# Gate and value in PSUM: three one-bank tiles in place of three slices of one tile, with a newly searched order

## The chip, the cores and the metric

The kernel runs on one core of one Trainium2 chip. The metric is the device time of one execution in microseconds (us). The time before is the median of three runs, 1481.7 us (1477.79 to 1482.69).

## What is computed

Three layers over 8192 tokens of 192 features, in float32:

```
w   = softmax(weight_gen)                        # per token, head and tap: 8 heads, 7 taps
x   = sum over taps of w * x at earlier tokens   # causal dynamic convolution
h   = x @ w_in                                   # 192 -> 2048
g   = (a0 + a1 h + a2 h^2 + a3 h^3) / (1 + |b0||h| + |b1| h^2 + 1e-6)
y   = g @ w_out                                  # 2048 -> 192
xn  = y / sqrt(mean(y^2) + 1e-6) * rms_g
out = (silu(xn @ w_gate) * (xn @ w_val)) @ w_out2   # 192 -> 1536 -> 192
```

## The kernel before, in words

The tokens are worked in 32 blocks (`b`) of 256 tokens. Products that need float32 are made from two float16 halves, so that one product of 192 features is five matmuls (`mm5`, line 837), and one of the second matrices three.

A block has two parts.

- **Rational part**, four quarters `q` of 512 columns each. `mm1` writes one PSUM tile `h` of two banks (two such tiles exist). ScalarE squares it (`tB`) and takes `|h|` (`tA`). VectorE makes the cubic in place in `h` (lines 875, 879), forms `g1h` (884) and the remainder (898), GpSimd forms `g1l` (902). The denominator is summed in one of three ways, chosen per quarter by the table `VAR` under `("qp", q)`: way 0 on VectorE (862), then ScalarE (889) and GpSimd (895); way 1 with one more ScalarE pass (856), then GpSimd (860) and GpSimd (895); way 2 on VectorE twice (862, 893). `mm2` multiplies `g1h` and `g1l` into the one bank `acc`.
- **Gate and value part**, six pieces `k` of 256 columns for gate and for value. `mm3` (ten matmuls at line 837) writes one bank of `gv`. There are three such banks, and the groups take them in turn, the gate and the value groups together. For a gate group ScalarE reads the bank with Silu and writes `gp` in SBUF (`silu`, line 984). For a value group VectorE multiplies bank and `gp` (`prod`, line 999); for four of the six pieces the product stays in the bank, ScalarE rounds it to float16 (`prod_hi`, line 1003) and VectorE takes the remainder (`prod_lo`, line 1007). After that the bank is free. `mm4` (line 1022) multiplies `gp` into `acc`.

Around these two parts GpSimd multiplies taps and inputs for the convolution of later blocks (373, 395), ScalarE makes the norm (925 to 957), and the first 140 us decode and split the weights. Silu and the exponentials need different ScalarE tables: a change between them is an ACT_TABLE_LOAD, issued ahead of a Silu or of an Ln.

Every engine takes its instructions in the order in which they were recorded. That order is a list of numbers, `RANK`, one per job (4777 jobs), found by a search outside the kernel. The waits between engines are set by the layer that records the program, by the tiles that instructions read and write. The search's own table of places, `CAPS`, counts three places for `gv`, before and after.

The lines that matter here:

```
late["gv"] = ... .tile([128, 3, NJ, 256], FP32, name="gv")     # gv_open, NJ = 2
gv[b, k, nm] = late["gv"][:, len(gv) % 3]                       # mm3
nc.scalar.activation(out=gp[b, k], in_=gv[b, k, "g"], func=ACTF.Silu, scale=silu_s)
nc.vector.tensor_tensor(out=l, in0=gv[b, k, "v"][:, 0:n16(k)], in1=h, op=ALU.subtract)
```

Of the kernel before, what the change touches and what calls it, by code (L numbers as in the profile page):

```python
# [10 lines left out]
FP32 = mybir.dt.float32  # L11
# [8 lines left out]
PSUM = bass.MemoryType.PSUM  # L20
# [3 lines left out]
def kernel(  # L24
# [31 lines left out]
    NJ = N2 // NK  # L56
# [69 lines left out]
    def c1(name):  # L126
# [702 lines left out]
    late = {}  # L829
# [141 lines left out]
    def gv_open():  # L971
        dec_ctx.__exit__(None, None, None)
        late["gv"] = ctx.enter_context(tc.tile_pool(name="ps_g", bufs=1, space=PSUM)).tile([128, 3, NJ, 256], FP32, name="gv")

    gv = {}

    def mm3(b, k, nm):
        gv[b, k, nm] = late["gv"][:, len(gv) % 3]
        for j in range(NJ):
            mm5(gv[b, k, nm][:, j, :], w3[nm, "A"], w3[nm, "B"], w3[nm, "C"], NJ * k + j, xnT[b])  # L980
# [49 lines left out]
    def store_out(b):  # L1030
# [507 lines left out]
```

## Time and profile before

| what | value |
|---|---|
| median of three runs | 1481.7 us |
| the profiled execution's own time | 1478.36 us |
| its span, first to last instruction | 1476.5 us |
| TensorE (PE) busy | 1248.8 us, 85% |
| VectorE (DVE) busy | 1222.8 us, 83% |
| ScalarE (ACT) busy | 1111.8 us, 75% |
| GpSimd (POOL) busy | 992.1 us, 67% |
| DMA engines busy, queue q1 | 12.8% |

The span runs from the first to the last instruction, the execution's own time is 1.9 us longer. The view by line gives for each group of instructions the busy time, the mean duration of one, the idle time of its engine just before them, and the engine and line that ended most of that idle time. The chain of work is followed back from the last instruction, at each step to what released it.

### The profile page before, as it was taken

The page shows a single profiled execution, that of the slowest core. Times are in us where ns is not written, and L with a number is a line of the kernel's source. Part 1 is how long each engine was busy: PE and PEld are TensorE (multiplying, and loading weights), DVE is VectorE, ACT ScalarE, POOL GpSimd, SP SyncE. Part 2 cuts the span into 40 slices and gives each one's busy share as a digit, 9 for nine tenths or more (in the row PEclk, how much of TensorE's full clock was granted, in tenths as well). Part 3 has the DMA queues.
Part 4 walks back from the last instruction along what each step waited for, and adds up shares of the span by engine and source line. Part 5 has one row for each costly group of instructions (what it writes and reads, how often), then busy time and mean ns, then how long its engine had stood idle before and what let it go on. Part 6 is the DMA issues. An engine that isn't in the chain of part 4 may idle for free.

```text
span 1476.5 us, 28197 instructions
## 1 busy us (share of the span) xinstructions
PE 1248.8 (85%) x11696; PEld 1122.1 (76%) x11696; DVE 1222.8 (83%) x1265; ACT 1111.8 (75%) x1521; POOL 992.1 (67%) x885
## 2 busy tenths in 40 slices
PE   3556788888899898998998888989888999988986
PEld 3455677777788787888887777878887888987876
DVE  5898788788888888978898979889887998987732
ACT  5878778777778778777787877778777888877832
POOL 6397678587857687776767677677665758675410
PEclk9887999999999999999999999999999999999999
DMA  7504420000002011002000021001010100000000
GB/s 256 166 22 97 112 90 18 20 20 17 12 9 60 15 49 31 12 15 60 14 15 15 7 63 18 15 21 33 28 25 7 26 12 23 17 18 12 17 7 16
DMA packets 69662, 55.02 MB, mean 37 GB/s; under 512 B 53791, under 2 KB 64543, under 8 KB 68638
## 3 DMA queue, kind: packets, MB, share of 16 engines
q1 hardware_dynamic: 66846, 49.18, 12.8%
q10 hardware_dynamic: 2688, 4.05, 0.8%
q8 instruction: 91, 1.49, 0.4%
q14 instruction: 37, 0.30, 0.1%
HBM read 31.72 MB, written 6.29 MB: 26 GB/s over the span
## 4 chain that ended last, share of the span: by engine, by line
PE 47%; DVE 23%; ACT 20%; issue 4%; POOL 4%; DMA 2%; DVEq 0%; SPq 0%; ACTq 0%; POOLq 0%
PE gv L837 23%; PE h L837 10%; ACT gp L984 6%; PE acc L1022 5%; DVE gv L999 3%; DVE tA L862 3%; DVE gp L1007 3%; PE acc L918 2%; PE acc L920 2%; PE acc L919 2%; DVE h L879 2%; DVE tA L898 2%; DVE g1h L884 2%; ACT gp L1003 2%; DVE h L875 2%
## 5 line engine op out<-in xcount | busy, mean ns | idle before, releaser
L902 POOL TENSOR_TENSOR g1l<-tA,tC 128x1024 f16<-128x1024 f32 x128 | 309.7, 2419 | 131.3 <-DVE tA L898 81.4
L918 PE MATMUL acc<-wo1h,g1h 128*128 128x192 f16 x992 | 245.9, 248 | 9.6 <-ACT y L925 6.7
L920 PE MATMUL acc<-wo1h,g1l 128*128 128x192 f16 x992 | 245.7, 248 | 7.1 <-POOL g1l L902 7.1
L919 PE MATMUL acc<-wo1l,g1h 128*128 128x192 f16 x992 | 245.8, 248 | 0.0
L837 PE MATMUL h<-xt,w1A 128*128 128x256 f16 x1024 | 221.4, 278 | 28.4 <-DVE tA L898 25.3
L837 PE MATMUL gv<-xnT,w3vA 128*128 128x256 f16 x768 | 174.6, 274 | 69.7 <-ACT gp L984 19.2
L837 PE MATMUL gv<-xnT,w3gA 128*128 128x256 f16 x768 | 170.3, 273 | 63.7 <-ACT gp L984 37.4
L1022 PE MATMUL acc<-wo,gp 128*128 128x192 f16 (+1 forms) x1920 | 221.8, 267 | 2.6 <-ACT osb L1028 2.5
L373 POOL TENSOR_TENSOR pt<-xc,wg 128x384 f32<-128x384 f32 x224 | 212.0, 991 | 1.4 <-DVE ac L389 0.5
L837 PE MATMUL h<-xt,w1C 128*128 128x256 f16 x1024 | 200.0, 278 | 0.0
L984 ACT ACTIVATE gp<-gv,silu_s 128x512 f32<-128x512 f32 x192 | 125.3, 686 | 94.3 <-PE gv L837 85.1
L884 DVE SCALAR_TENSOR_TENSOR g1h<-h,cf,tC 128x1024 f16<-128x1024 f32 x128 | 163.8, 1279 | 35.3 <-ACT tC L871 29.9
L875 DVE SCALAR_TENSOR_TENSOR h<-tB,cf,h 128x1024 f32<-128x1024 f32 x128 | 163.9, 1280 | 11.3 <-ACT tA L851 10.9
L898 DVE SCALAR_TENSOR_TENSOR tA<-h,cf,tA 128x1024 f32<-128x1024 f32 x128 | 163.6, 1278 | 3.1 <-POOL tA L895 1.4
L879 DVE SCALAR_TENSOR_TENSOR h<-tB,cf,h 128x1024 f32<-128x1024 f32 x128 | 164.0, 1281 | 1.9
L999 DVE SCALAR_TENSOR_TENSOR gv<-gp,val_h,gv 128x512 f32<-128x512 f32 x128 | 96.2, 752 | 68.1 <-PE gv L837 48.8
L851 ACT ACTIVATE tA<-h,cf 128x1024 f32<-128x1024 f32 x128 | 141.9, 1108 | 12.8 <-POOL g1l L902 6.0
L895 POOL TENSOR_TENSOR tA<-tA,g1h 128x1024 f32<-128x1024 f32 x54 | 115.4, 2138 | 51.2 <-DVE g1h L884 45.7
L871 ACT ACTIVATE tC<-tC,lnb 128x1024 f32<-128x1024 f32 x128 | 146.5, 1145 | 2.8
L837 PE MATMUL gv<-xnT,w3vC 128*128 128x256 f16 x768 | 147.6, 274 | 0.0
L837 PE MATMUL gv<-xnT,w3gC 128*128 128x256 f16 x768 | 147.0, 273 | 0.0
L847 ACT ACTIVATE tB<-h 128x1024 f32<-128x1024 f32 x128 | 129.9, 1015 | 20.8 <-PE h L837 20.7
(227 smaller groups left out, 3136.8 us busy)
## 6 DMA issues: line engine op xcount, KB each, us to landing
xc<-in_x_dram SPq DMA_DIRECT2D x7, 1344.0 KB, 6.4
out_dram<-osb SPq DMA_DIRECT2D x32, 192.0 KB, 2.0
xp<-in_x_dram SPq DMA_DIRECT2D x14, 384.0 KB, 3.3
raw<-in_moe_w_in_dram SPq DMA_DIRECT2D x6, 512.0 KB, 7.0
raw<-in_moe_w_out_dram SPq DMA_DIRECT2D x3, 768.0 KB, 4.5
wg<-in_weight_gen_dram SPq DMA_DIRECT2D x15, 112.0 KB, 2.0
raw<-in_moe_w_out_dram ACTq DMA_DIRECT2D x2, 768.0 KB, 8.6
raw<-in_moe_w_gate_dram SPq DMA_DIRECT2D x2, 768.0 KB, 4.9
```

The source lines that it names most:

```text
L373: nc.gpsimd.tensor_tensor(out=pt_t[b][:, :, :, k].rearrange("p i (h g) -> p i h g", h=NH), in0=xc_t[k0][:, o0 + k:o0 + k + 2, :].rearrange ...
L837: nc.tensor.matmul(out=dst, lhsT=w[:, fs], rhs=xt[:, :, c, :], start=(n == 0), stop=(n == 4))
L875: nc.vector.scalar_tensor_tensor(out=h, in0=tB[q], scalar=cf[:, 4:5], in1=h, op0=ALU.add, op1=ALU.mult)
L879: nc.vector.scalar_tensor_tensor(out=h, in0=tB[q], scalar=cf[:, 5:6], in1=h, op0=ALU.mult, op1=ALU.add)
L884: nc.vector.scalar_tensor_tensor(out=g1h[q], in0=hps[q], scalar=cf[:, 3:4], in1=tC[q], op0=ALU.add, op1=ALU.mult)
L898: nc.vector.scalar_tensor_tensor(out=tA[q], in0=hps[q], scalar=cfb(q)[:, 3:4], in1=tA[q], op0=ALU.add, op1=ALU.subtract)
L902: nc.gpsimd.tensor_tensor(out=g1l[q], in0=tA[q], in1=tC[q], op=ALU.mult)
L918: nc.tensor.matmul(out=acc[:, 0:D], lhsT=g1h[q][:, r, ts], rhs=wo1h[:, f, :], start=(f == 0), stop=False)
L919: nc.tensor.matmul(out=acc[:, 0:D], lhsT=g1h[q][:, r, ts], rhs=wo1l[:, f, :], start=False, stop=False)
L920: nc.tensor.matmul(out=acc[:, 0:D], lhsT=g1l[q][:, r, ts], rhs=wo1h[:, f, :], start=False, stop=(f == N1 - 1))
L984: nc.scalar.activation(out=gp[b, k], in_=gv[b, k, "g"], func=ACTF.Silu, scale=silu_s)
L1022: nc.tensor.matmul(out=acc[:, 0:D], lhsT=l, rhs=r, start=(f == 0 and n == 0), stop=(f == N2 - 1 and n == len(ops) - 1))
```

## The change

`gv_open` makes three tiles `gv0`, `gv1`, `gv2` of one bank each, where one tile `gv` of three banks stood, and `mm3` picks one of three tiles in place of one of three slices. The banks are as many and as large as before. `RANK` has new numbers, and `VAR` new ways for 17 quarters.

```
     def gv_open():
         dec_ctx.__exit__(None, None, None)
-        late["gv"] = ctx.enter_context(tc.tile_pool(name="ps_g", bufs=1, space=PSUM)).tile([128, 3, NJ, 256], FP32, name="gv")
+        pool = ctx.enter_context(tc.tile_pool(name="ps_g", bufs=1, space=PSUM))
+        late["gv"] = [pool.tile([128, NJ, 256], FP32, name=f"gv{i}") for i in range(3)]
...
     def mm3(b, k, nm):
-        gv[b, k, nm] = late["gv"][:, len(gv) % 3]
+        gv[b, k, nm] = late["gv"][len(gv) % 3]
...
-    RANK = [24, 28, 30, 37, 40, 44, 49, 56, 58, 61, 62, 63, 69, 73, 79, 82, 70, 80, 84, 91, 93, 94, 27, 32, 35, 39,
...
```

In `VAR` the quarters change as follows (old way, new way): 15, 70, 84: 0, 1; 25, 37, 43, 65: 2, 0; 38, 94: 1, 0; 56, 111: 0, 2; 92, 98, 106, 127: 2, 1; 96, 124: 1, 2. In all way 0 goes from 15 quarters to 16, way 1 from 39 to 42, way 2 from 74 to 70. The entry `('way', 'last')` that is added changes no instruction. Lines from 974 on stand one line lower in the changed kernel (984 is 985, 999 is 1000, 1003 is 1004, 1007 is 1008, 1500 is 1501).

The instructions that differ in number, counted in the recorded programs: line 856 and line 866 on ScalarE 39 to 42, line 868 there 89 to 86, line 889 there 15 to 16; table loads 47 to 50 ahead of Silu and 46 to 49 ahead of Ln; on VectorE line 862 89 to 86, line 893 74 to 70; on GpSimd line 860 39 to 42, line 895 54 to 58. All else is as many as before.

The order on VectorE at the end of the program, last two blocks, with the engine each row waits for (`gv_1118` is the one tile with three banks, `gv0` to `gv2` the three tiles; the names of `gp` buffers are numbered through). Before:

```order
L999 SCALAR_TENSOR_TENSOR gv_1118<-gp_16378,val_h_142,gv_1118 128x512 [waits Activation_49]
L1007 TENSOR_TENSOR gp_16368<-gv_1118,gp_16368 128x512 [waits DVE_49]
L999 SCALAR_TENSOR_TENSOR gv_1118<-gp_16429,val_h_142,gv_1118 128x512 [waits DVE_49,PE_49]
L1007 TENSOR_TENSOR gp_16429<-gv_1118,gp_16429 128x512 [waits Activation_49]
L1007 TENSOR_TENSOR gp_16378<-gv_1118,gp_16378 128x512 [waits Activation_49]
...
L999 SCALAR_TENSOR_TENSOR gv_1118<-gp_16717,val_h_142,gv_1118 128x512 [waits DVE_49,PE_49]
L1007 TENSOR_TENSOR gp_16717<-gv_1118,gp_16717 128x512 [waits PE_49,Activation_49]
```

and now:

```order
L1000 SCALAR_TENSOR_TENSOR gv0_1049<-gp_16437,val_h_142,gv0_1049 128x512 [waits PE_49]
L1008 TENSOR_TENSOR gp_16437<-gv0_1049,gp_16437 128x512 [waits Activation_49]
L1000 SCALAR_TENSOR_TENSOR gv2_1051<-gp_16450,val_h_142,gv2_1051 128x512 [waits PE_49]
L1008 TENSOR_TENSOR gp_16450<-gv2_1051,gp_16450 128x512 [waits Activation_49]
...
L1000 SCALAR_TENSOR_TENSOR gv0_1049<-gp_16753,val_h_142,gv0_1049 128x512 [waits PE_49]
L1008 TENSOR_TENSOR gp_16761<-gv2_1051,gp_16761 128x512 [waits Activation_49]
L1008 TENSOR_TENSOR gp_16753<-gv0_1049,gp_16753 128x512 [waits Activation_49]
```

`prod_lo` needs only `prod_hi` of ScalarE on its own bank. Before, 26 of its 128 instructions also wait for TensorE, which writes another bank; now none does. Of `prod_hi`, which needs only `prod` of VectorE, 51 of 128 waited for TensorE before and 3 do now.

The order on ScalarE some 45 rows before the end, around the last Silu of block 29. Before:

```order
L868 ACTIVATE tC_16271<-tA_16235,cf1_132 128x1024 [waits DVE_49]
L1003 ACTIVATE gp_16025<-gv_1118 128x512 [waits DVE_49,PE_49]
L871 ACTIVATE tC_16271<-tC_16271,lnb_160 128x1024 [waits Activation_49]
L1028 ACTIVATE osb_16057<-acc_16226,out_s_144 128x192 [waits PE_49]
L984 ACT_TABLE_LOAD [waits DVE_49]
L984 ACTIVATE gp_16340<-gv_1118,silu_s_141 128x512 [waits PE_49]
L984 ACTIVATE gp_16355<-gv_1118,silu_s_141 128x512 [waits DVE_49,PE_49]
L984 ACTIVATE gp_16368<-gv_1118,silu_s_141 128x512 [waits PE_49]
```

and now:

```order
L985 ACT_TABLE_LOAD [waits DVE_49]
L985 ACTIVATE gp_16336<-gv1_1050,silu_s_141 128x512 [waits PE_49]
L1501 ACT_TABLE_LOAD
L866 ACTIVATE tC_16291<-tA_16299 128x1024 [waits Pool_49]
L871 ACTIVATE tC_16291<-tC_16291,lnb_160 128x1024 [waits Activation_49]
L985 ACT_TABLE_LOAD
L985 ACTIVATE gp_16412<-gv1_1050,silu_s_141 128x512 [waits PE_49]
L985 ACTIVATE gp_16415<-gv0_1049,silu_s_141 128x512 [waits DVE_49]
```

Here one Silu is taken ahead of the last Ln and Exp, at two more table loads. The last quarter has gone from way 2 to way 1.

The first Silus of block 31, the last block, on the same engine, before:

```order
L984 ACTIVATE gp_16681<-gv_1118,silu_s_141 128x512 [waits PE_49]
L984 ACTIVATE gp_16693<-gv_1118,silu_s_141 128x512 [waits PE_49]
L984 ACTIVATE gp_16705<-gv_1118,silu_s_141 128x512 [waits PE_49]
L984 ACTIVATE gp_16717<-gv_1118,silu_s_141 128x512 [waits PE_49]
L1028 ACTIVATE osb_16719<-acc_16371,out_s_144 128x192 [waits DMAHW4_49]
```

and now:

```order
L985 ACTIVATE gp_16710<-gv1_1050,silu_s_141 128x512 [waits PE_49]
L985 ACTIVATE gp_16722<-gv0_1049,silu_s_141 128x512 [waits DVE_49]
L1004 ACTIVATE gp_16722<-gv2_1051 128x512 [waits DVE_49]
L985 ACTIVATE gp_16753<-gv1_1050,silu_s_141 128x512 [waits PE_49]
L985 ACTIVATE gp_16761<-gv0_1049,silu_s_141 128x512
```

Before, six Silus stood in a row, the first four of block 31 last among them; now a value piece's `prod_hi` (line 1004) is taken between the gates.

## Rows read from the trace of the kernel before

**Rows 1.** The page, part 1: busy time of the engines over the span.

```profile
PE 1248.8 (85%) x11696; PEld 1122.1 (76%) x11696; DVE 1222.8 (83%) x1265; ACT 1111.8 (75%) x1521; POOL 992.1 (67%) x885
```

**Rows 2.** The page, part 4: the chain that ended last, by line.

```profile
PE gv L837 23%; PE h L837 10%; ACT gp L984 6%; PE acc L1022 5%; DVE gv L999 3%; DVE tA L862 3%; DVE gp L1007 3%; PE acc L918 2%; PE acc L920 2%; PE acc L919 2%; DVE h L879 2%; DVE tA L898 2%; DVE g1h L884 2%; ACT gp L1003 2%; DVE h L875 2%
```

**Rows 3.** The view by line, the groups around `gv` and `h`.

```profile
L837 PE MATMUL h<-xt,w1A 128*128 128x256 f16 x1024 | 221.4, 278 | 28.4 <-DVE tA L898 25.3 <-ACT h L512 2.8
...
L837 PE MATMUL gv<-xnT,w3vA 128*128 128x256 f16 x768 | 174.6, 274 | 69.7 <-ACT gp L984 19.2 <-DVE gp L1007 17.8 <-DVE gv L999 15.6
L837 PE MATMUL gv<-xnT,w3gA 128*128 128x256 f16 x768 | 170.3, 273 | 63.7 <-ACT gp L984 37.4 <-DVE gp L999 16.7 <-DMA xnT<-xn 4.8
...
L984 ACT ACTIVATE gp<-gv,silu_s 128x512 f32<-128x512 f32 x192 | 125.3, 686 | 94.3 <-PE gv L837 85.1 <-DVE gp L999 7.4 <-DVE gp L1007 1.2
```

**Rows 4.** Waits: engine, line, what was waited for: us in total, times, longest.

```profile
ACT gp L1003 <- PE gv L837: 24.8, 25, 2.6
...
DVE gp L1007 <- PE gv L837: 12.7, 14, 2.1
```

**Rows 5.** The view of tile `gv`: who waited for its users (us, times).

```profile
  PE gv L837: 127.0, 149
```

**Rows 6.** Timeline of TensorE: start, length, instruction, idle before; block 0 and block 31.

```profile
155.32 0.27 PE L837 MATMUL gv<-xnT,w3gA 128*128 128x256 f16 x1 [0.78 <-ACT gp L984]
...
1438.19 0.27 PE L837 MATMUL gv<-xnT,w3gA 128*128 128x256 f16 x1 [0.78 <-ACT gp L984]
...
1439.17 0.27 PE L837 MATMUL gv<-xnT,w3gA 128*128 128x256 f16 x1
1440.22 0.27 PE L837 MATMUL gv<-xnT,w3gA 128*128 128x256 f16 x1 [0.78 <-ACT gp L984]
...
1463.49 0.27 PE L837 MATMUL gv<-xnT,w3vA 128*128 128x256 f16 x1 [1.04 <-ACT gp L1003]
```

**Rows 7.** Timeline of ScalarE beside it, block 31.

```profile
1437.46 0.69 ACT L984 ACTIVATE gp<-gv,silu_s 128x512 f32<-128x512 f32 x1 [1.34 <-PE gv L837]
1439.48 0.69 ACT L984 ACTIVATE gp<-gv,silu_s 128x512 f32<-128x512 f32 x1 [1.34 <-PE gv L837]
```

**Rows 8.** Busy time by stage: start:end, length, PE, PEld, DVE, ACT, POOL, then clock.

```profile
0.00:140.00 140.00, 71.44 (x494) 62.65 (x495) 114.66 (x176) 102.82 (x127) 93.18 (x88) 0.85 0.45 138
140.00:300.00 160.00, 134.01 (x1193) 116.03 (x1191) 133.28 (x171) 122.25 (x164) 114.61 (x96) 0.94 0.23 59
300.00:1300.00 1000.00, 898.13 (x8656) 813.37 (x8654) 871.70 (x818) 786.45 (x1081) 719.07 (x646) 1.00 0.10 24
1200.00:1300.00 100.00, 95.32 (x936) 87.57 (x935) 88.49 (x82) 87.19 (x116) 70.36 (x61) 1.00 0.06 15
1300.00:1476.50 176.50, 145.20 (x1362) 130.02 (x1359) 103.14 (x103) 100.30 (x151) 65.28 (x58) 0.99 0.06 14
```

**Rows 9.** The view by line, what the new ways of the quarters add and remove.

```profile
L862 DVE SCALAR_TENSOR_TENSOR tA<-tB,cf,tA 128x1024 f32<-128x1024 f32 x89 | 133.7, 1503 | 6.2 <-ACT tA L851 3.7 <-ACT tB L847 2.4
...
L895 POOL TENSOR_TENSOR tA<-tA,g1h 128x1024 f32<-128x1024 f32 x54 | 115.4, 2138 | 51.2 <-DVE g1h L884 45.7 <-ACT tA L889 5.3
L893 DVE SCALAR_TENSOR_TENSOR tA<-tA,cf,g1h 128x1024 f32<-128x1024 f32 x74 | 105.6, 1426 | 1.5
...
L860 POOL TENSOR_TENSOR tA<-tA,tC 128x1024 f32<-128x1024 f32 x39 | 92.0, 2359 | 67.8 <-ACT tC L856 53.2 <-ACT tA L851 14.3
...
L1500 ACT ACT_TABLE_LOAD x46 | 59.0, 1283 | 0.8
...
L856 ACT ACTIVATE tC<-tB,cf 128x1024 f32<-128x1024 f32 x39 | 48.3, 1239 | 1.4 <-POOL g1l L902 0.9
...
L889 ACT ACTIVATE tA<-tA,cf 128x1024 f32<-128x1024 f32 x15 | 17.1, 1143 | 0.2
```

**Rows 10.** One line's instructions, VectorE 862 and 898: duration in ns, min/median/max.

```profile
L862 DVE SCALAR_TENSOR_TENSOR tA<-tB,cf,tA x89: 1256/1284/3391, 58.5 to 1393.7; 128x1024 f32<-128x1024 f32 x89
...
L898 DVE SCALAR_TENSOR_TENSOR tA<-h,cf,tA x128: 1185/1279/1285, 65.8 to 1409.5; 128x1024 f32<-128x1024 f32 x128
```

572 rows, old and new, of tables (RANK, VAR) are left out of this document.

## The prediction
> **What bounds the kernel now.** I read the page first. No engine is full: TensorE is busy 85% of the span, VectorE 83%, ScalarE 75%, GpSimd 67% [rows 1]. The stages say where: TensorE has 71.4 of the first 140 us, 134.0 of the next 160, 898.1 of the 1000 us from 300 to 1300, and 145.2 of the last 176.5 [rows 8]. In the long middle no other engine is closer to full: VectorE 871.7, ScalarE 786.5, GpSimd 719.1 of 1000.
>
> Then the chain of waits: TensorE's `gv` groups hold 23% of it, with the three readers of `gv` at 6, 3, 3 and 2% (Silu, `prod`, `prod_lo`, `prod_hi`) [rows 2]. So the chain runs again and again from TensorE through a reader of `gv` back to TensorE. The view by line gives the price on TensorE: 69.7 us idle before value groups and 63.7 before gate groups, 133.4 in all, against 28.4 before the `h` groups [rows 3]. Of it, 127.0 us in 149 places waited for a reader of `gv` [rows 5].
>
> **Are these waits for the bank that is needed?** Three banks should let TensorE fill one while the others are read. In block 31 they don't. A gate group starts at 1438.19, its last matmul at 1439.17; Silu starts at 1439.48; the next gate group starts at 1440.22, after 0.78 us idle that ended with that Silu [rows 6, 7]. Silu's own idle time of 1.34 us ended with TensorE. The two engines strictly alternate, at 2.03 us a step (1438.19 to 1440.22), as if there were one bank. The bank taken at 1440.22 was last read three groups earlier and was long free.
>
> Two more rows cannot come from the right bank at all: `prod_hi` waits 24.8 us for TensorE, `prod_lo` 12.7 us [rows 4], though each needs only the step before it on VectorE or ScalarE. The recorded order agrees: 51 and 26 of 128 of them carry a wait for TensorE, since the waits go by the tile and the three banks are one tile.
>
> **The change, part by part.**
>
> *Three tiles.* With a tile per bank, a group waits only for the readers of the group three before it. I went through the 384 groups and took, for each, its start less the later of two ends, each with 0.06 us for the hand-over: that of the matmul ahead, and that of the last reader of its own bank. In 152 places the group starts later than both; the sum is 95.8 us: nothing before 140 us, 11.5 (19 places) from 140 to 300, 63.1 (106) from 300 to 1300, 21.2 (27) after. The first over half a microsecond is at 155.32, the last at 1463.49 [rows 6]. The other 37 or so of the 133.4 us are true waits for a bank, hand-overs and the transposed input's DMA. So this term is **-95.8 us** on TensorE's path. Its bounds: 0, if another wait takes its place each time, and -133.4, if all idle time before `gv` goes.
>
> *What is late next.* The middle would then last 1000 - 63.1 = 936.9 us with TensorE at 898.1 / 936.9 = 95.9%. The row nearest to that is the stretch from 1200 to 1300, where TensorE already reaches 95.3% with VectorE at 88.5% and ScalarE at 87.2% [rows 8]. So the kernel can feed TensorE at that rate. VectorE would be at some 92%, ScalarE at 85%, GpSimd at 78%. They too lose the false waits (the 37.5 us above among them), so I give nothing back.
>
> *The new ways of 17 quarters.* VectorE loses three instructions of line 862 at 1.503 us and four of line 893 at 1.426: -10.2 us. GpSimd gains three of line 860 at 2.359 and four of line 895 at 2.138: +15.6. ScalarE gains three of line 856 at 1.239, one of 889 at 1.143, and six table loads at 1.283: +12.6 [rows 9]. All of it lies beside TensorE in the middle, ScalarE and GpSimd having over 130 us idle there after the cut. I take 0, with -10 (VectorE's share on the path) and +13 (ScalarE's) as bounds. No DMA and no matmul is added or removed.
>
> *The new order.* It moves jobs on every engine, and the trace of before has no row for it. In the first 140 us the same decoding has to be done, with TensorE idle 68.6 us; one tenth of that either way, 7 us, is my bound. At the end, Silus and values alternate where six Silus stood in a row; the false waits there are already counted. I take 0.
>
> **Sum.** The profiled execution took 1478.4 us, 1.9 more than its span; 1478.4 - 95.8 = 1382.6. The median of the runs is 3.3 us higher, so for the median 1481.7 - 95.8 = 1385.9: I forecast **1386 us**, 6.5% less. Its own range is 1366 to 1406: the bounds of ways and order added, 20 either way.
>
> **A rule against it.** Line 862, two inputs in SBUF, has a median of 1.284 us but a mean of 1.503 and a maximum of 3.391, while line 898, one input in PSUM, never exceeds 1.285 [rows 9, 10]. Over 89 and 74 instructions of lines 862 and 893 that is some 30 us above the median. The Trainium skill (SBUF — State Buffer, section Who interferes with whom) says that a VectorE instruction with two SBUF inputs contends with a GpSimd instruction that reads SBUF; the rows agree. By that rule a denser schedule stretches VectorE more: with the 30 us grown as GpSimd's share does, from 72 to 78%, the sum would be some 2 us higher, and 30 us higher if they doubled. I leave it out of the sum.
>
> **Rivals.**
>
> *A: derived waits go as well (0.17).* VectorE's and ScalarE's delays also make TensorE wait for `h`. From 1200 to 1300, 3.1 of TensorE's 4.7 idle us are false waits by the count above; without them it would be busy 98.4%. With that in the whole middle, 898.1 / 0.984 = 912.7, a gain of 87.3, with 11.5 and 21.2 from the other stages 120: 1362 us. For it: `RANK` was searched with three free places, which the program has only now. Against: VectorE would have to reach 95%.
>
> *B: VectorE becomes the bound (0.20).* If VectorE keeps the 88.5% of that best stretch, the middle lasts (871.7 - 10.2) / 0.885 = 973 us, a gain of 27; with 11.5 and 21.2 it is 59: 1422 us. For it: VectorE is nearly as busy as TensorE, and its stretched instructions above. Against: part of VectorE's own idle time is false waits too, 12.7 us at `prod_lo` alone [rows 4].
>
> *C: slower (0.04).* The wait moves on to `h`, and ScalarE comes on the path: TensorE's idle time before `h` [rows 3] would grow from 28 to over 120 us, all that is gained at `gv`, because every `h` is freed only after ScalarE's Ln and Exp. Then ScalarE's added 12.6 us count in full: 1481.7 + 12.6 = 1494. It decides if ScalarE is above some 90% in the middle; it stands at 79% [rows 8], which speaks against.
>
> *D: no change (0.04).* The waits stay, under another name, 1482. The recorded order speaks against: no `prod_lo` waits for TensorE any more, and 3 of 128 `prod_hi`.
>
> **How the numbers follow.** The forecast has 0.55. Faster by over 0.3%, about what a measurement of this kernel can tell from no change: forecast, A and B, 0.92. Within it: D, 0.04. Slower: C, 0.04. The range goes from 1345 (A less VectorE's 10 us and 7 of the start) to 1430 (B with some 8 us, most of ScalarE's added work); C, D and the tails beyond A and B, in all about 2 in 10, are outside.
>
> **What would show it.** Right: TensorE's idle time before `gv` at 30 to 50 us instead of 133; no row of `prod_hi` or `prod_lo` waiting for TensorE above 2 us; in the last block, gate groups that follow each other in under 1.3 us where no `mm4` stands between; TensorE at 95 to 97% from 300 us on. A shows as over 97% there. B shows as TensorE waiting for `h` from line 898 for 60 us or more, VectorE below 90%. The forecast is wrong if the wait before `gv` falls below 50 us and the time does not fall by 59 us, or if it stays above 100.

## The result and the profile after

The changed kernel takes 1321.1 us (1319.4 to 1323.6, four runs) against 1479.7 us before: ratio 0.8928, 95% interval 0.8902 to 0.8954. It is 159 us faster. The forecast was 1386 us with a range of 1345 to 1430; the direction and the mechanism were right, the size was not, and the time lies 24 us below the range.

The profiled execution has a span of 1321.6 us, 154.9 less than before. Busy time and chain on the page, which answer to [rows 1, 2]:

```profile
PE 1223.5 (93%) x11696; PEld 1120.1 (85%) x11696; DVE 1207.8 (91%) x1258; ACT 1115.7 (84%) x1531; POOL 1025.8 (78%) x892
...
PE gv L837 19%; PE h L837 12%; PE acc L1023 8%; PE acc L918 4%; PE acc L920 4%; PE acc L919 4%; POOL g1l L902 3%; DVE tA L862 3%; DVE tA L898 2%; DVE g1h L884 2%; DMA xnT<-xn 2%; DVE h L875 2%; ACT tC L871 2%; ACT tA L851 2%; DVE tA L893 2%
```

The four readers of `gv`, which held 14% of the chain, are gone from its first lines. The view by line of the same kernel answers to [rows 3]; the columns are busy time, mean ns | idle time before, and what ended it:

```profile
L837 PE MATMUL h<-xt,w1A 128*128 128x256 f16 x1024 | 223.6, 281 | 28.7 <-DVE tA L898 22.0 <-ACT h L512 2.8 <-DMA xt<-hl 1.8
...
L837 PE MATMUL gv<-xnT,w3vA 128*128 128x256 f16 x768 | 170.7, 273 | 2.4 <-DVE gp L1008 2.0 <-ACT gp L985 0.2
L837 PE MATMUL gv<-xnT,w3gA 128*128 128x256 f16 x768 | 164.6, 273 | 7.9 <-DMA xnT<-xn 7.8
...
L985 ACT ACTIVATE gp<-gv,silu_s 128x512 f32<-128x512 f32 x192 | 124.9, 692 | 20.5 <-PE gv L837 19.5
```

The view of tile `gv` (who waited for its users: us, times) answers to [rows 5]:

```profile
  PE gv L837: 2.2, 4
```

TensorE's idle time before the `gv` groups has gone from 133.4 to 10.3 us, and 7.8 of these wait for the transposed input, not for a bank. Of waits for a reader of `gv`, 2.2 us in 4 places are left of 127.0 in 149. The stages answer to [rows 8] (start:end, length, then busy PE, PEld, DVE, ACT, POOL, and TensorE's clock); the middle now ends at 1200:

```profile
0.00:140.00 140.00, 75.52 (x498) 63.23 (x498) 113.65 (x176) 103.44 (x127) 93.02 (x87) 0.78 0.48 140
140.00:300.00 160.00, 143.82 (x1335) 128.40 (x1336) 148.88 (x185) 138.44 (x188) 130.38 (x112) 0.96 0.24 61
300.00:1200.00 900.00, 886.69 (x8709) 819.09 (x8708) 865.93 (x818) 789.71 (x1092) 755.09 (x653) 1.00 0.11 26
...
1200.00:1321.60 121.60, 117.42 (x1159) 109.44 (x1156) 79.37 (x82) 84.06 (x126) 47.34 (x43) 1.00 0.08 18
```

From 300 to 1200 us TensorE is busy 98.5% and VectorE 96.2%. In the last blocks groups follow each other without a stop between them. The timeline of TensorE and of ScalarE (start, length, instruction, idle before):

```profile
1260.83 0.27 PE L837 MATMUL gv<-xnT,w3vA 128*128 128x256 f16 x1
...
1261.92 0.27 PE L837 MATMUL gv<-xnT,w3gA 128*128 128x256 f16 x1
...
1263.01 0.27 PE L837 MATMUL gv<-xnT,w3vA 128*128 128x256 f16 x1
...
1264.11 0.27 PE L837 MATMUL gv<-xnT,w3gA 128*128 128x256 f16 x1
```

```profile
1271.05 0.69 ACT L985 ACTIVATE gp<-gv,silu_s 128x512 f32<-128x512 f32 x1 [0.79 <-PE gv L837]
1272.14 0.69 ACT L985 ACTIVATE gp<-gv,silu_s 128x512 f32<-128x512 f32 x1 [0.41 <-PE gv L837]
```

A group starts every 1.09 us, where before the two engines took turns at 2.03 us [rows 6, 7]; in the last block two gate groups in a row start at 1299.18 and 1300.27 us. Silu still waits for TensorE, but for the group it reads.

### The profile page after: what moved, and what is told of

Same layout as the page of the kernel before. It is cut to its first block, busy times and chain, and to the rows that moved or that the text cites. A ratio compares the mean times of both kernels' runs of the same rounds, so it can differ in the third digit from the quotient of the medians.

```text
span 1321.6 us, 28151 instructions
## 1 busy us (share of the span) xinstructions
PE 1223.5 (93%) x11696; PEld 1120.1 (85%) x11696; DVE 1207.8 (91%) x1258; ACT 1115.7 (84%) x1531; POOL 1025.8 (78%) x892
## 3 DMA queue, kind: packets, MB, share of 16 engines
q1 hardware_dynamic: 66846, 49.18, 14.6%
## 4 chain that ended last, share of the span: by engine, by line
PE 53%; DVE 17%; ACT 12%; POOL 10%; DMA 4%; issue 4%; SPq 0%; POOLq 0%; DVEq 0%; ACTq 0%
PE gv L837 19%; PE h L837 12%; PE acc L1023 8%; PE acc L918 4%; PE acc L920 4%; PE acc L919 4%; POOL g1l L902 3%; DVE tA L862 3%; DVE tA L898 2%; DVE g1h L884 2%; DMA xnT<-xn 2%; DVE h L875 2%; ACT tC L871 2%; ACT tA L851 2%; DVE tA L893 2%
## 5 line engine op out<-in xcount | busy, mean ns | idle before, releaser
L837 PE MATMUL h<-xt,w1A 128*128 128x256 f16 x1024 | 223.6, 281 | 28.7 <-DVE tA L898 22.0
L373 POOL TENSOR_TENSOR pt<-xc,wg 128x384 f32<-128x384 f32 x224 | 225.8, 1053 | 0.8
L837 PE MATMUL gv<-xnT,w3vA 128*128 128x256 f16 x768 | 170.7, 273 | 2.4 <-DVE gp L1008 2.0
L837 PE MATMUL gv<-xnT,w3gA 128*128 128x256 f16 x768 | 164.6, 273 | 7.9 <-DMA xnT<-xn 7.8
L895 POOL TENSOR_TENSOR tA<-tA,g1h 128x1024 f32<-128x1024 f32 x58 | 126.6, 2183 | 24.3 <-DVE g1h L884 21.7
L837 PE MATMUL h<-xt,w1B 128*128 128x256 f16 x512 | 144.0, 281 | 0.0
L837 PEld LDWEIGHTS <-w1A 128*128 128x128 f16 x1024 | 103.0, 101 | 46.9 <-DVE tA L898 28.5
```

What stands on the lines that cost most here:

```text
L373: nc.gpsimd.tensor_tensor(out=pt_t[b][:, :, :, k].rearrange("p i (h g) -> p i h g", h=NH), in0=xc_t[k0][:, o0 + k:o0 + k + 2, :].rearrange ...
L837: nc.tensor.matmul(out=dst, lhsT=w[:, fs], rhs=xt[:, :, c, :], start=(n == 0), stop=(n == 4))
```

## The experiments

The question was where 155 us of span come from when 95.8 were counted: from the three tiles alone, whose removal of delays reaches further than the count (S), or from the tiles and the new order together (O).

**1. The three tiles alone.** The kernel before, with its order and its ways of the quarters; of the change it has only the new lines in `gv_open` and `mm3`.

> The kernel before with the three tiles alone; order and ways of the quarters as before. Theory S (the split alone gave nearly all of the 158 us, more than the 96 us counted, because every delay of TensorE, ScalarE and VectorE that hung on it goes too): 1315 to 1350 us, TensorE idle before the gv groups 10 to 30 us. Theory O (the split gives the 96 us that were counted and the new order the other 60): 1375 to 1395 us, TensorE idle before gv 30 to 50 us. Halfway, some 1360, would mean both.

Measured: 1323.6 us, ratio 0.8951 (0.8927 to 0.8974). That is theory S. The busy line and the view by line of this kernel:

```profile
PE 1221.6 (92%) x11696; PEld 1121.5 (85%) x11696; DVE 1211.1 (92%) x1265; ACT 1103.9 (84%) x1521; POOL 1003.6 (76%) x885
```

```profile
L837 PE MATMUL h<-xt,w1A 128*128 128x256 f16 x1024 | 220.2, 277 | 19.2 <-DVE tA L898 15.8 <-ACT h L512 2.8
...
L837 PE MATMUL gv<-xnT,w3vA 128*128 128x256 f16 x768 | 171.3, 273 | 2.6 <-DVE gp L1008 1.8 <-ACT gp L985 0.9
L837 PE MATMUL gv<-xnT,w3gA 128*128 128x256 f16 x768 | 166.5, 275 | 12.0 <-DMA xnT<-xn 5.9 <-DVE gp L1008 3.3 <-DVE gp L1000 1.6
```

Since order and ways are those of before, this run is the clean comparison; the mean granted clock is 0.978 in both profiles. Its span of 1321.1 us is 155.4 shorter, and TensorE's account of it closes: idle time before `gv` 133.4 to 14.6, -118.8; idle time before `h` 28.4 to 19.2, -9.2; busy time 1248.8 to 1221.6, -27.2, with the same 11696 matmuls. Together these are 155.2.

**2. The order and the ways alone.** The changed kernel with one tile and three slices put back.

> The changed kernel with one tile and three slices again; new order and new ways stay. Theory S: the order is worth little by itself, 1465 to 1500 us, TensorE idle before gv again 120 to 140 us. Theory O: the order is worth 60 us with or without the split, 1410 to 1430 us.

Measured: 1484.4 us, ratio 1.0035 (1.0019 to 1.0051). Its busy line and the `gv` groups in the view by line:

```profile
PE 1249.3 (84%) x11696; PEld 1120.7 (76%) x11696; DVE 1216.6 (82%) x1258; ACT 1121.9 (76%) x1531; POOL 1023.6 (69%) x892
```

```profile
L837 PE MATMUL gv<-xnT,w3vA 128*128 128x256 f16 x768 | 174.9, 275 | 62.2 <-DVE gp L1007 19.9 <-ACT gp L984 19.2 <-ACT gp L1003 11.8
L837 PE MATMUL gv<-xnT,w3gA 128*128 128x256 f16 x768 | 170.0, 274 | 66.8 <-ACT gp L984 38.4 <-DVE gp L999 17.8 <-DVE gp L1007 4.2
```

That is theory S again: the 129.0 us of idle time before `gv` and the 1249 us of busy time are back together. Without the tiles the new order with its ways is slightly worse than the old, by 0.35%.

**3. The new order with the old ways.** The changed kernel with the table `VAR` of before.

> The changed kernel with the old ways of the 17 quarters; tiles and order new. VectorE gets 10 us of work back, GpSimd loses 16 and ScalarE 5 (the six table loads belong to the order and stay). If the ways are beside TensorE's work, as the prediction has it: within 4 us of the changed kernel, 1317 to 1325. If VectorE, 96% busy from 300 us on, is on the path too: 1328 to 1335.

Measured: 1338.7 us, ratio 0.9051 (0.9027 to 0.9075): 17.6 us over the changed kernel, more than either expectation. TensorE's idle time before `h` rises from 28.7 to 35.2 us, that before `gv` is 11.2 where it was 10.3:

```profile
L837 PE MATMUL h<-xt,w1A 128*128 128x256 f16 x1024 | 221.2, 278 | 35.2 <-DVE tA L898 28.1 <-DMA xt<-hl 3.0 <-ACT h L512 2.8
```

**4. The old order with the new ways,** on three tiles.

> The kernel before with the three tiles and the new ways of 17 quarters; the order stays old. If the new ways are better in themselves (VectorE has 10 us less to do and is over 95% busy in the middle): 1305 to 1320 us, faster than the three tiles alone (1323.6). If order and ways fit only each other, as the loss of 17 us with the new order and the old ways suggests: 1328 to 1345 us.

Measured: 1342.3 us, ratio 0.9077 (0.9055 to 0.9098), 18.7 us over the three tiles with old order and old ways, though VectorE has 7.9 us less to do than there (1203.2 against 1211.1). TensorE's idle time before `h` is 25.6 us where it was 19.2, and before `gv` 22.8 where it was 14.6:

```profile
L837 PE MATMUL h<-xt,w1A 128*128 128x256 f16 x1024 | 221.3, 278 | 25.6 <-DVE tA L898 21.8 <-ACT h L512 2.8 <-DMA xt<-hl 0.5
...
L837 PE MATMUL gv<-xnT,w3vA 128*128 128x256 f16 x768 | 171.3, 273 | 6.0 <-DVE gp L1008 5.1 <-ACT gp L985 0.9
L837 PE MATMUL gv<-xnT,w3gA 128*128 128x256 f16 x768 | 166.4, 275 | 16.8 <-DMA xnT<-xn 7.8 <-DVE gp L1008 3.7 <-ACT gp L985 3.4
```

Neither set of ways is better by itself: mixing order and ways costs 1.3 to 1.4% in both directions. That the search had fitted the two to each other is the likely reason, but no run shows it. Where in the program those 18 us arise was not followed further.

**5. Both kernels on one chip.** The three tiles with the old order, and the changed kernel, each run again with five rounds.

> The kernel before with the three tiles alone, again, beside the changed kernel on the same chip: 1323 us (1321 to 1326), that is 0.1 to 0.4% over the changed kernel if the new order with its ways is worth anything at all, the same if not.

> The changed kernel again, on the same chip as the three tiles alone: 1320 to 1323 us. Both at the same time would mean that order and ways together are worth nothing.

Measured: 1323.6 us, ratio 0.8952 (0.8925 to 0.8979), and 1322.3 us, ratio 0.8944 (0.8925 to 0.8962). They are 1.4 us apart, and the intervals lie on each other: order and ways, searched further, gave nothing that these runs can tell from zero. Within that, the whole gain is the tiles'.

**6. One pair of banks tied.** The changed kernel, with two of the three banks as slices of one tile:

```
-        late["gv"] = [pool.tile([128, NJ, 256], FP32, name=f"gv{i}") for i in range(3)]
+        g0 = pool.tile([128, NJ, 256], FP32, name="gv0")
+        g12 = pool.tile([128, 2, NJ, 256], FP32, name="gv12")
+        late["gv"] = [g0, g12[:, 0], g12[:, 1]]
```

> The changed kernel with bank 0 as a tile of its own and banks 1 and 2 as two slices of one tile: of the three pairs of banks one still waits for each other. If the cost goes with the number of tied pairs: a third of 158 us comes back, 1365 to 1385 us, TensorE idle before gv some 45 us. If one free neighbour is enough to keep TensorE fed: below 1345 us.

> The changed kernel with banks 0 and 1 as two slices of one tile and bank 2 alone, the other pair than in the run with two tiles (1357.1 us). If a tied pair costs the same wherever it stands: 1350 to 1365 us, TensorE idle before gv 28 to 38 us in 45 to 65 breaks. If it hangs on which groups of the order meet in the pair: outside 1345 to 1370.

The second run has `[g12[:, 0], g12[:, 1], g0]`. Measured: 1357.1 us, ratio 0.9176 (0.9153 to 0.92), and 1361.8 us, ratio 0.9212 (0.9194 to 0.923). The `gv` groups by line, two rows of the first run and two of the second (lines from 974 on stand three lower than in the kernel before, so that 984 is 987):

```profile
L837 PE MATMUL gv<-xnT,w3vA 128*128 128x256 f16 x768 | 171.7, 272 | 17.0 <-ACT gp L987 5.5 <-DVE gp L1010 5.3 <-ACT gp L1006 3.8
L837 PE MATMUL gv<-xnT,w3gA 128*128 128x256 f16 x768 | 165.3, 273 | 15.8 <-ACT gp L987 5.7 <-DMA xnT<-xn 4.4 <-DVE gp L1002 4.3
```

```profile
L837 PE MATMUL gv<-xnT,w3vA 128*128 128x256 f16 x768 | 171.9, 274 | 16.9 <-DVE gp L1010 7.0 <-ACT gp L987 4.8 <-ACT gp L1006 2.6
L837 PE MATMUL gv<-xnT,w3gA 128*128 128x256 f16 x768 | 165.3, 273 | 16.9 <-ACT gp L987 8.7 <-DMA xnT<-xn 4.2 <-DVE gp L1002 3.2
```

One tied pair of three costs 36 and 41 us, about a quarter of what three tied pairs cost (163 us, from experiment 2 to the changed kernel). For the first run it was neither the third that was expected nor the little that one free neighbour would leave; the second lies where a tied pair was expected to cost the same wherever it stands, 5 us from the first. The third pair was not run. From one tied pair to three the cost rises faster than the number of ties.

**7. What bounds the changed kernel.** Two kernels that leave work out: one without the matmuls of line 919, one without the instructions of line 879.

```
...
-            nc.tensor.matmul(out=acc[:, 0:D], lhsT=g1h[q][:, r, ts], rhs=wo1l[:, f, :], start=False, stop=False)
```

> The changed kernel without the 1024 matmuls of line 919 (the product of g1h with the low half of w_out is left out of y). TensorE has 1024 x 0.082 = 84 us less to do, nearly all of it from 140 us on. If TensorE alone bounds the changed kernel (98.5% busy from 300 to 1200 us): 1235 to 1250 us. If VectorE, 96% busy there, is the next bound close behind, it can give up only its 4% of some 1000 us and the start's waits: 1275 to 1300 us.

```
     def dve_p2(q):
-        h, cf = hps[q], cfb(q)
-        nc.vector.scalar_tensor_tensor(out=h, in0=tB[q], scalar=cf[:, 5:6], in1=h, op0=ALU.mult, op1=ALU.add)
+        return
```

> The changed kernel without the 128 instructions of line 879 on VectorE (the quadratic term is left out of the cubic): VectorE has 164 us less to do. If TensorE alone bounds: its idle time of 22 us before h (line 898) and some of the start go, 1295 to 1318 us. If VectorE bounds as much as TensorE does: the same, since TensorE stays where it is; a gain of over 35 us would mean that VectorE, not TensorE, bounds.

Measured: 1315.0 us and 1320.9 us, ratios 0.8875 (0.8839 to 0.8912) and 0.8916 (0.887 to 0.8962). The middle of both by stage, first without line 919, then without line 879:

```profile
300.00:1200.00 900.00, 837.57 (x7963) 758.11 (x7961) 868.78 (x821) 790.77 (x1097) 762.58 (x654) 1.00 0.11 26
```

```profile
300.00:1200.00 900.00, 886.61 (x8715) 819.99 (x8715) 756.61 (x723) 789.39 (x1093) 761.83 (x653) 1.00 0.11 26
```

and the longest wait of TensorE without line 919, then of VectorE without line 879 (engine, line, waited for: us, times, longest; without line 879 what was line 884 is line 883):

```profile
PE h L837 <- DVE tA L898: 53.1, 37, 6.4
```

```profile
DVE g1h L883 <- ACT tC L871: 93.0, 73, 3.1
```

Without some 84 us of TensorE's work the kernel gains 6 us, which two runs hardly tell from nothing: TensorE falls to 93% and waits 53.1 us for `h` from line 898, where it waited 22.0, while VectorE is at 96.5%. Both expectations for that run are missed; why VectorE gave up none of its last 4% is open. Without 164 us of VectorE's work the kernel gains nothing, as expected if both engines bound: VectorE falls to 84% and TensorE stays at 98.5%. So in this order, which was made for the full work, the two engines are both nearly full, and the time stays when either one is relieved.

## Why the prediction was wrong in size

**Right.** The waits before `gv` were for banks that were free, and they went with the tiles: by experiment 1 the tiles give the whole gain, by experiment 2 the rest of the change gives none without them. Of the signs set down for it two are there: no wait of `prod_hi` or `prod_lo` for TensorE, and gate groups 1.09 us apart. Two went further than forecast: 10 us before `gv` where 30 to 50 were named, and TensorE at 98.5% where 95 to 97 were. The latter is rival A's sign. Rival B's is absent (22.0 us before `h`, VectorE 96.2%), and C and D are out. Order and ways together were taken at 0, and experiment 5 shows 0.

**The step that failed** is the first term of the sum, -95.8 us, "the other 37 or so of the 133.4 us are true waits for a bank, hand-overs and the transposed input's DMA". Experiment 1 has 155 in its place, in three parts.

- Of the 37 us only 14.6 stay. The rest were mostly waits for the right bank, but for a reader that was itself late. In the trace of before, 49 groups waited for their own bank, 31.8 us in all. In 39 of them, 26.3 us, a reader of that bank had started late although its engine was idle and its input ready, that is, it had stood in a false wait; in experiment 1 no reader does, and 6.7 us in 10 places are left. Counting each group's delay against the reader's actual end books such a wait as true. The bound of -133.4 stood beside it and was nearer. (The count itself takes the readers in the order of the pieces. The recorded order differs in places, for 53 of the 192 Silus; with the readers taken by it the 95.8 us in 152 places become 91.7 in 147, a little further off.)
- TensorE's busy time was taken as work that stays, 898.1 us in the middle. It is not: the profile shows a matmul with a length of 0.27 us, and within a group the next one starts 0.11 us after it (ten from 1438.19 to 1439.17 [rows 6]); only the last one before a stop adds its full length to the busy time, some 0.16 us more than the others. Between the kernel before and experiment 1 TensorE's stretches of idle time, the stops, fall from 225 to 70, and its busy time by 27.2 us, which is 0.175 us for each stop that went. The two kernels run the same matmuls in the same order, so they can be set side by side: in the 162 places where only the kernel before stops, the time from one start to the next falls by 140.8 us, of which 115.2 were shown as idle and 25.6, 0.158 each, as busy. Experiment 2 shows the opposite: 216 stops, 1249.3 us.
- The wait before `h` fell by 9.2 us, once the false waits were gone from VectorE too. That is rival A's mechanism; the sum gave it nothing.

**No ceiling.** The middle came out at 95.9%, and the best stretch of before, at 95.3% [rows 8], was taken to confirm it. But that stretch held false waits too, so it showed what the kernel could do with them, not without. Rival A saw this, and its 98.4% is what came; it still arrived at 1362 us, since it too kept 898.1 us of work and, outside the middle, the count's 11.5 and 21.2 us. Its objection, that VectorE would have to reach 95%, was no objection: VectorE reaches 96.2%, and rival B's 88.5% was a share that VectorE had while it waited, not one it could not exceed.

**The ways** were costed at 0 with bounds of -10 and +13. They are worth 17.6 us with the new order and cost 18.7 us with the old one (experiments 3 and 4), both outside those bounds. The new order was taken at 0 by itself as well; with the old ways it costs 15.1 us (1338.7 against 1323.6). That the two cancel, as the forecast's 0 for both needs, is luck.

**The rule against it.** Line 862 now takes 1.536 us in the mean and line 893 1.422, against 1.503 and 1.426 [rows 9], with GpSimd at 755 of 900 us in the middle, 84% where it had 72:

```profile
L862 DVE SCALAR_TENSOR_TENSOR tA<-tB,cf,tA 128x1024 f32<-128x1024 f32 x86 | 132.1, 1536 | 7.3 <-ACT tA L851 5.6 <-ACT tB L847 1.4
...
L893 DVE SCALAR_TENSOR_TENSOR tA<-tA,cf,g1h 128x1024 f32<-128x1024 f32 x70 | 99.6, 1422 | 1.8
```

The Trainium skill (SBUF — State Buffer, section Who interferes with whom) speaks of contention between such instructions and GpSimd's reads. The traces show these instructions hardly longer in sum: some 31 us above the 1.284 us of [rows 10], where there were 30, with seven instructions fewer. So leaving it out of the sum did no harm.

## What to carry to other kernels

When several PSUM banks are meant to be filled and read in turn, make each a tile of its own, and look in the recorded order for waits on an engine that does nothing to the bank in question: one tile over three banks cost this kernel a tenth of its time. Here false waits cost more than their own length on the engine that showed them: count also the waits they make elsewhere and, for each stop, the part that stands in TensorE's busy time. In this kernel all idle time before the groups, 133.4 us, was a better estimate than the waits counted one by one, and still too low. The best stretch of a trace with the fault in it is no ceiling for the kernel without it.

## What was not expected of the hardware

TensorE and VectorE ran at 98.5% and 96.2% side by side for 900 us, with ScalarE at 88% and GpSimd at 84%, and reads of one bank beside writes to another lengthened hardly anything: Silu takes 692 ns where it took 686. TensorE's busy time for the same 11696 matmuls was 1249 us with 216 to 225 stops and 1222 us with 70, at a mean granted clock of 0.974 to 0.978 in each of these three executions.
